# Block 0 of x loaded as plain rows and transposed on TensorE, in a gated attention and token-MLP kernel

## The chip, the cores and the metric

The kernel runs on one core of a Trainium2 chip. The metric is the device time in microseconds (us) of one execution; of several runs the median counts. The core has five engines with instruction streams of their own: TensorE (PE in the profile, PEld for its weight loads), VectorE (DVE), ScalarE (ACT), GpSimd (POOL) and SyncE (SP). SP and ACT also issue DMA transfers.

## The reference, cut to what matters

```python
x = A_x                                        # (1, 2048, 512) bf16
g = sigmoid((x * gate_w).sum(-1, keepdims=True))
qkv = x @ wqkv                                 # 512 -> 3*512, 32 heads of 16
# each position attends to 8 positions: itself and 2, 4, .. 14 before it
a = softmax(q . k[pos - 2w], masked where pos - 2w < 0) . v[pos - 2w] @ wo
h = layernorm(x, axis=-1)                      # over the 512 channels
u = gelu(einsum("bsd,sf->bdf", h, w1) + b1)    # token mixing, F = 1792
y = einsum("bdf,fs->bds", u, w2) + b2
out = g * a + (1 - g) * transpose(y)
```

The matmuls are the projections of q, k and v, the two of the token MLP, the output projection, and small ones that sum products over a head.

## The kernel before, in words

The sequence of 2048 positions is cut into 16 tiles of 128 (t, or st) and into 4 blocks of 512 (sb). Block 0 is tiles 0 to 3. x is held in SBUF twice. `X` has positions on the partitions and is used for the layernorm and the MLP. `XT` has channels on the partitions: four channel groups dt of 128, each 2048 positions long; it is the moving operand of the q, k and v projections.

**How the order is made.** Nothing is executed where it is written. `A` (`_Sched.add`, L88) and `sch.dma` (L114) record operations with an engine, a planned duration, and the names that they read and write. `_pass` (L146) is a list scheduler: it gives each engine a fixed order from planned durations. A DMA's end is planned from its bytes (L210 to L213), or set by hand in `lands` (L214). `chain(...)` (L924) forces an order on the operations named. `plan_waits` (L235) turns dependencies into semaphore waits. At run time each engine follows its list; an operation whose operands are late holds up all that stands behind it on that engine. [...]

**The start.** GpSimd writes a tile of ones (L421) and makes the identity matrix from it (L422). VectorE clears a tile, `warm0` (L525), and sums the identity to the indicator `RP` (L429). TensorE runs nine matmuls of that zero tile, `warm1` (L527 to L535), 128x512 each. Their result is used by nothing.

Meanwhile ACT's queue loads the first channel group of q's weights (`ld_w(0, 0, 1, "act")`, 128 KB), and SP's queue issues in this order (L477 to L491): two transposing loads that fill `XT` for positions 0 to 383 and 384 to 511 (`ld_xt0`, L472); channel group 1 of q's weights (128 KB); groups 2 and 3 (256 KB); all of k's weights (512 KB); a transposing load of block 1 (`ld_xt`, L465); X tiles 0 to 3 and 4 to 7 (`ld_x`, 512 KB each); the transposing loads of blocks 2 and 3; X tiles 8 to 11 and 12 to 15; v's weights. From there on a load waits until the fifth load before it in a list has landed (`throttle`, L438).

**Projections of block 0** (L613 to L619). q has four outputs (dl 0 to 3) in PSUM banks 0 to 3, k has four in banks 4 to 7. TensorE runs for the four q banks: channel group 0 for positions 0 to 383 (four 128x384 matmuls), group 0 for 384 to 511 (four 128x128), group 1 (four 128x512), groups 2 and 3 (eight 128x512). Then come the four k banks (sixteen 128x512). Here "the k projections" means those sixteen. After them TensorE goes on with blocks 1 to 3, v, and so on (L623 to L637). ScalarE copies each finished bank to SBUF (L606, L609).

**After the projections.** VectorE multiplies q by shifted k (`qkm`, L668), and TensorE sums the products over heads (`qkr`, L676), in bursts of 32 matmuls put between its other work. Layernorm statistics are `ln1` (L553, one per tile) and `ln2`; ScalarE normalises (`ln3`, L577). The MLP's matmuls are L794 and L844. The softmax follows on VectorE and ScalarE, then the weighted sum of v (L779 to L784), then the output projection on TensorE (`wo`, L860) and the combination on VectorE (`cmb`, L881). VectorE's order is written out in one chain (L940 to L946): `warm0`, `rp`, statistics of tiles 0 to 3, `qkm_0_0_0`, `qkm_0_1_0`, statistics of tiles 4 to 7, and so on.

Of the kernel before, what the change touches and what calls it, by code (L numbers as in the profile page):

```python
# [27 lines left out]
OUTQ = "sp"  # L28
XS = 384
HT0 = 12  # L30


class _Op:
# [256 lines left out]
def _views(nc, es):  # L290
    off = {}
    cur = [0]

    def region(name, nbytes):
        nbytes = (nbytes + 63) // 64 * 64
        off[name] = cur[0]
        cur[0] += nbytes

    region("X", NST * D * 2)
    region("XT", 4 * S * 2)  # L300
    region("WQKV", 4 * 3 * D * 2)
    region("W1W", 4 * NST * 256 * 2)
    region("PBUF", 2 * 4 * S * 2)
    region("WO", 4 * D * 2)
    region("Q5", 4 * S * 2)
    region("K5", 4 * KROW * 2)
    region("V5", 4 * KROW * 2)
    region("ATX", 8 * NW * HC * 2)
    region("ATT", NW * SC * 2)
    region("OUTS", 4 * D * 2)  # L310
    region("BR", 128)
    region("BT", 128)
    region("IDENT", 128 * 2)
    region("ONES", 128 * 2)
    region("RP", 32 * 2)
    region("SMALL", 2048)
    total = cur[0]
    arena = es.enter_context(nc.sbuf_tensor("arena", [128, total], U8))

    def view(name, dtype, dims, extra=0):  # L320
        base = arena[:].bitcast(dtype)
        pstride = base.ap[0][0]
        esz = mybir.dt.size(dtype)
        assert off[name] % esz == 0
        return bass.AP(base.tensor, off[name] // esz + extra, [[pstride, 128]] + [list(d) for d in dims])

    def pview(name, dtype, p0, np_, dims, extra=0):
        base = arena[:].bitcast(dtype)
        pstride = base.ap[0][0]
        esz = mybir.dt.size(dtype)  # L330
        return bass.AP(base.tensor, p0 * pstride + off[name] // esz + extra, [[pstride, np_]] + [list(d) for d in dims])

    return view, pview, off, total


def bass_gated_mix__sliding_local_dilated__mixer_token_mlp__prompt_kernel(nc, A_x, A_wqkv, A_wo, B_x, B_w1, B_b1, B_w2, B_b2, gate_w, out, dbg=None):
    with contextlib.ExitStack() as es:
# [32 lines left out]
        ATT = view("ATT", BF16, [(NW * HC, 2), (HC, NW), (1, HC)])  # L370
        T1 = view("X", BF16, [(D, NST), (1, D)])
        IDENT = view("IDENT", BF16, [(1, 128)])
        ONES = view("ONES", BF16, [(1, 128)])
        RP = view("RP", BF16, [(1, 32)])
        M4 = view("PBUF", FP32, [(4 * HC, 2), (HC, 4), (1, HC)], extra=0)
        M2 = view("PBUF", FP32, [(2 * HC, 2), (HC, 2), (1, HC)], extra=8 * HC)
# [38 lines left out]
        def psub(ap_, p0, np_, offs, dims):  # L415
# [2 lines left out]

        A = sch.add

        c_ones = A("pool", lambda e: e.memset(ONES, 1.0), 0.3, writes=["ones"], name="ones")  # L421
        c_ident = A("pool", lambda e: e.affine_select(out=IDENT, in_=ONES, pattern=[[1, 128]], compare_op=ALU.is_equal,  # L422
                                                     fill=0.0, base=0, channel_multiplier=-1),
                    0.4, reads=["ones"], writes=["ident"], name="ident")
        A("pool", lambda e: e.memset(sub(K5, 0, [(KROW, 4), (1, PAD)]), 0.0), 0.2, writes=["k5pad"], name="k5pad")
        A("pool", lambda e: e.memset(sub(V5, 0, [(KROW, 4), (1, PAD)]), 0.0), 0.2, writes=["v5pad"], name="v5pad")
        def f_rp(e):
# [5 lines left out]
        def mk_dma(dst, src):  # L433
            return lambda e: e.dma_start(dst, src)  # L434
# [17 lines left out]
        def ld_w(tn, d0, n, q="sp"):  # L452
            ds = sch.dsem("wqkv%d_%d" % (tn, d0))
            op = sch.dma(q, mk_dma(WQKV[:, d0:d0 + n, tn * D:(tn + 1) * D], wqkv_v[:, d0:d0 + n, tn * D:(tn + 1) * D]),
                         n * 128 * D * 2, ds, writes=["wqkv%d_%d" % (tn, dt) for dt in range(d0, d0 + n)],
                         deps=throttle() if q == "sp" and n == 4 else [], after=prev_dma() if q == "sp" else [],
                         issue=0.65 if n == 4 else 0.45, name="d_wp%d_%d" % (tn, d0))
            if q == "sp":
                init_dmas.append(op)
            return op  # L460
# [8 lines left out]
        def ld_xt0(s0, s1):  # L469
            ds = sch.dsem("xt0_%d" % s0)  # L470
            dst = XT[:, :, s0:s1]
            op = sch.dma("sp", lambda e: e.dma_start_transpose(dst, x2d[s0:s1, :]), (s1 - s0) * D * 2, ds, issue=1.25,  # L472
                         writes=["xt_%d" % t for t in range(s0 // 128, s1 // 128)], after=prev_dma(), name="d_xt0_%d" % s0)
            init_dmas.append(op)
            return op

        first_loads = [ld_w(0, 0, 1, "act"), ld_xt0(0, XS), ld_xt0(XS, 512), ld_w(0, 1, 1), ld_w(0, 2, 2), ld_w(1, 0, 4)]  # L477
        for op_ in first_loads[4:]:
            op_.deps -= set(init_dmas)
        ld_xt(1)  # L480
        init_dmas[-1].deps -= set(init_dmas)
        for op_, t_ in zip(first_loads + [init_dmas[-1]], (2.3, 3.95, 4.5, 4.8, 5.6, 7.2, 9.2)):
            op_.lands = t_
        del init_dmas[2]
        ld_x(0, 4)
        ld_x(4, 4)
        ld_xt(2)
        ld_xt(3)
# [32 lines left out]
        A("act", lambda e: e.activation(out=B1C, in_=BT[:, 0, 0:NFT], func=AF.Copy), 0.2, reads=["btc"], writes=["b1c"], name="b1c")  # L521
        A("act", lambda e: e.activation(out=B2C, in_=BT[:, 1, 0:NST], func=AF.Copy), 0.2, reads=["btc"], writes=["b2c"], name="b2c")

        WARM = view("OUTS", BF16, [(1, D)], extra=0)
        A("dve", lambda e: e.memset(WARM, 0.0), 0.2, writes=["outs0"], name="warm0")  # L525

        def f_warm(n):  # L527
            def fn(e):
                ins = None
                for _ in range(n):  # L530
                    ins = e.matmul(ps[:, 7, :], lhsT=WARM[:, 0:128], rhs=WARM, start=True, stop=True)
                return ins
            return fn

        last_tx = A("pe", f_warm(9), 4.0, reads=["outs0"], writes=["lg7_0", "lg7_1"], name="warm1", prio=-100)  # L535

        ALLXT = ["xt_%d" % t for t in range(NST)]

        JK = view("OUTS", BF16, [(1, D)], extra=0)
        def cols(v_, lo, n, step=1):  # L540
# [9 lines left out]
        for hf in range(2):  # L550
            t0 = 8 * hf
            for t in range(t0, t0 + 8):
                A("dve", (lambda t_: (lambda e: e.bn_stats(out=ST6[:, t_, :], in_=X[:, t_, :])))(t), 0.59,  # L553
                  reads=["x%d" % t], writes=["st6_%d" % t], name="ln1_%d" % t, prio=0)
            sr = ["st6_%d" % t for t in range(t0, t0 + 8)]
            h8 = (lambda v_: cols(v_, t0, 8))
            A("dve", (lambda t0_: (lambda e: e.tensor_tensor(out=mv(t0_, 0, 2), in0=st6(t0_, 1, 8, 2), in1=st6(t0_, 4, 8, 2), op=ALU.add)))(t0),
# [53 lines left out]
        tnames = ["q", "k", "v"]  # L611
        first = [(tn, dl) for tn in range(2) for dl in range(4)]
        fbn = [["acc%d" % b] for b in range(4)] + [["lg%d_0" % b, "lg%d_1" % b] for b in range(4, 8)]  # L613
        for (b0, d0, d1, s0, s1) in ((0, 0, 1, 0, XS), (0, 0, 1, XS, 512), (0, 1, 2, 0, 512), (0, 2, 4, 0, 512), (4, 0, 4, 0, 512)):
            for b in range(b0, b0 + 4):
                tn, dl = first[b]
                last_main[0] = A("pe", f_proj(tn, dl, 0, b, d0, d1, s0, s1), 0.216 * (d1 - d0) * (s1 - s0) / 512,
                                 reads=ALLXT[s0 // 128:s1 // 128] + ["wqkv%d_%d" % (tn, dt) for dt in range(d0, d1)],
                                 writes=fbn[b], after=[last_main[0]], name="pf_%s%d_%d_%d" % (tnames[tn], dl, d0, s0))  # L619
        for b, (tn, dl) in enumerate(first):  # L620
            A("act", f_evq(tn, dl, 0, b), 0.52, reads=fbn[b] + (["k5pad"] if tn == 1 else []),
              writes=["%s5_%d_0" % (tnames[tn], dl)], name="ev_%s%d_0" % (tnames[tn], dl), prio=0)
# [188 lines left out]
        for ft in range(NFT):  # L811
            j = ft // 2
            emit_ph2(ft, (2, 3) if ft < 3 else (0, 1, 2, 3))
            bank = p2bank[ft]
            A("act", (lambda ft_, bank_: (lambda e: e.activation(out=UT[:, ft_, :], in_=ps[:, bank_, :], func=AF.Gelu_apprx_tanh,  # L815
                                                                bias=col(B1C, ft_))))(ft, bank), 0.72,
              reads=["acc%d" % bank, "b1c"], writes=["ut%d" % ft] + ALLXT,
              name="gel_%d" % ft, prio=0)
            if ft % 2 == 1 and j + 4 <= 6:
                ld_w1(j + 4)  # L820
# [103 lines left out]
        def chain(names):  # L924
            for a_, b_ in zip(names, names[1:]):
                byname[b_].order.add(byname[a_])

        def ln1(*ts):
            return ["ln1_%d" % t for t in ts]

        def ln2(hf):
            return ["ln2%s%d" % (c_, hf) for c_ in "abcd"]
# [4 lines left out]
        def lnr(hf):  # L937
            return ["ln_rstd%d" % hf, "ln_nmr%d" % hf]

        chain(["warm0", "rp"] + ln1(0, 1, 2, 3) + ["qkm_0_0_0", "qkm_0_1_0"] + ln1(4, 5, 6, 7) + ln2(0)  # L940
              + ["qkm_0_2_0"] + lnr(0) + ["qkm_0_3_0", "qkm_0_0_2"] + ln1(8, 9) + ["qkm_0_1_2"] + ln1(10, 11, 12) + ["qkm_0_2_2"] + ln1(13, 14)
              + ["qkm_0_3_2", "qkm_1_0_0"] + ln1(15) + ln2(1) + ["t_b", "qkm_1_1_0"] + lnr(1)
              + ["qkm_1_2_0", "msk_0", "sm_ma0", "sm_mb0", "qkm_1_3_0"] + gz(12, 13, 14, 15, 0, 1) + [
# [6 lines left out]
        def atn(u):  # L950
# [1 line left out]

        chain(["avm_2", "g_omg", "g_c2", "g_g", "ava_0"])
        chain(["ph3b_14"] + ["wo_%d" % i for i in range(4)] + ["ph3a_15", "ph3b_15", "wo_4"])
        chain(["ln3_%d" % t for t in range(8, 16)] + ["gel_0", "gel_1"] + ["lev_1_%d" % w for w in range(4)] + ["sm_pre", "sm_exp0", "sm_exp1", "gel_2", "gel_3", "gel_4"] + atn(0) + ["gel_5"] + atn(2) + ["gel_6"] + atn(1) + ["gel_7"] + atn(3)
              + ["gel_8", "g_tanh", "gel_9"] + atn(4) + ["gel_10"] + atn(6) + ["gel_11", "gel_12"] + atn(5) + ["gel_13"] + atn(7) + ["t1_0"])

        if dbg is not None and "keep" in dbg:
            keepf = dbg["keep"]
# [92 lines left out]
```

## Time and profile before

| | us |
|---|---|
| median of 3 runs | 170.05 |
| the runs | 169.89, 170.05, 170.68 |
| the profiled execution | 169.85 |
| its span, first to last instruction | 168.0 |

| engine | busy us | share of the span |
|---|---|---|
| PE | 163.9 | 98% |
| DVE | 150.8 | 90% |
| ACT | 75.5 | 45% |
| POOL | 1.0 | 1% |

A time in the profile counts from the first instruction. A `q` behind an engine's name (SPq, ACTq) means its instruction queue, where DMAs are issued. A matmul's listed duration runs past the start of the next one, since matmuls are pipelined; the distance from start to start is what one costs in a row of them. `x12` after a group is its number of instructions, and `[0.25 <-DMA ...]` is idle time before it and what ended that.

### The profile page before, as it was taken

What the parts mean: (1) busy time and instruction counts of PE and PEld (TensorE: products, weight loads), DVE (VectorE), ACT (ScalarE), POOL (GpSimd) and SP (SyncE); (2) the same over time, 40 slices, a digit from 0 to 9 for tenths busy, and PEclk for the clock granted to TensorE, in tenths of its full rate; (3) what the DMA queues carried; (4) which work ended last, traced back from release to release, by engine and by line L of the source; (5) the groups of instructions that cost most, each with busy time, mean ns of one, the idle gap of its engine ahead of it and who ended that gap; (6) DMA issues with size and microseconds to landing.
All of it is one profiled execution on the core that took longest, in us unless ns stands there. A gap on an engine that the chain in (4) does not pass through costs nothing.

```text
span 168.0 us, 2160 instructions
## 1 busy us (share of the span) xinstructions
PE 163.9 (98%) x861; PEld 77.4 (46%) x861; DVE 150.8 (90%) x154; ACT 75.5 (45%) x115; POOL 1.0 (1%) x9
## 2 busy tenths in 40 slices
PE   7999999999999999999999999999999999999993
PEld 2455555544454444444444444444444444444462
DVE  1009999999999998799999999999999999999995
ACT  3177788898979938791231221131221312310000
POOL 2000000000000000000000000000000000000000
PEclk9999999999999999999999999999999999999999
DMA  6899999956303999555889906472573470000554
GB/s 143 255 295 248 290 326 292 297 171 192 125 0 101 358 295 288 143 162 137 191 219 329 327 19 149 104 210 65 162 218 99 119 222 0 0 0 0 184 180 140
DMA packets 47593, 29.64 MB, mean 176 GB/s; under 512 B 9824, under 2 KB 46432, under 8 KB 47584
## 3 DMA queue, kind: packets, MB, share of 16 engines
q1 hardware_dynamic: 45760, 25.11, 54.2%
q10 hardware_dynamic: 1824, 4.39, 9.9%
q8 instruction: 7, 0.11, 0.3%
q14 instruction: 2, 0.02, 0.0%
HBM read 21.11 MB, written 2.10 MB: 138 GB/s over the span
## 4 chain that ended last, share of the span: by engine, by line
PE 92%; DVE 2%; SPq 2%; DMA 2%; issue 0%
PE ps L794 29%; PE ps L844 29%; PE ps L598 24%; PE ps L860 6%; PE ps L676 4%; DVE arena L881 2%; DMA arena<-in_A_wqkv_dram 2%; SPq L472 2%; SPq L434 0%
## 5 line engine op out<-in xcount | busy, mean ns | idle before, releaser
L794 PE MATMUL ps<-arena 128*128 128x512 bf16 x224 | 48.9, 379 | 0.0
L844 PE MATMUL ps<-arena 128*128 128x512 bf16 x224 | 48.7, 379 | 0.0
L598 PE MATMUL ps<-arena 128*128 128x512 bf16 (+2 forms) x196 | 42.2, 375 | 0.2 <-DMA arena<-in_A_wqkv_dram 0.2
L668 DVE TENSOR_TENSOR arena<-arena 128x4096 bf16<-128x4096 bf16 (+1 forms) x12 | 35.6, 2990 | 0.0
L779 DVE TENSOR_TENSOR arena<-arena 128x8192 bf16<-128x8192 bf16 x8 | 35.0, 4418 | 0.0
L794 PEld LDWEIGHTS ps<-arena 128*128 128x128 bf16 x224 | 21.8, 98 | 26.8 <-issue 0.8
L844 PEld LDWEIGHTS ps<-arena 128*128 128x128 bf16 x224 | 21.9, 98 | 26.4
L598 PEld LDWEIGHTS ps<-arena 128*128 128x128 bf16 x196 | 21.7, 113 | 20.8 <-DMA arena<-in_A_wqkv_dram 0.9
L911 ACT ACTIVATE arena<-ps,arena 128x512 bf16<-128x512 f32 x16 | 12.5, 778 | 39.4 <-PE ps L844 39.4
L782 DVE TENSOR_TENSOR arena<-arena 128x4096 bf16<-128x4096 bf16 (+1 forms) x16 | 27.0, 1751 | 0.0
L609 ACT ACTIVATE arena<-ps 128x512 bf16<-128x512 f32 x32 | 18.9, 596 | 5.4 <-PE ps L598 5.2
L815 ACT ACTIVATE arena<-ps,arena 128x512 bf16<-128x512 f32 x14 | 9.6, 688 | 24.7 <-PE ps L794 22.2
L553 DVE BATCH_NORM_STATS2 arena<-arena 128x6 f32<-128x512 bf16 x16 | 10.0, 680 | 11.2 <-DMA arena<-in_A_x_dram 11.2
L860 PE MATMUL ps<-arena 128*128 128x512 bf16 (+1 forms) x80 | 14.2, 336 | 0.0
L606 ACT ACTIVATE arena<-ps 128x512 bf16<-128x512 f32 x16 | 9.0, 597 | 7.2 <-PE ps L598 7.2
L577 ACT ACTIVATE arena<-arena 128x512 bf16<-128x512 bf16 x16 | 12.0, 804 | 0.0
L881 DVE SCALAR_TENSOR_TENSOR arena<-ps,arena 128x512 bf16<-128x512 f32 (+1 forms) x20 | 11.5, 637 | 0.4 <-PE ps L860 0.2
L860 PEld LDWEIGHTS ps<-arena 128*128 128x128 bf16 x80 | 7.8, 98 | 6.2
L652 DVE SCALAR_TENSOR_TENSOR arena<-arena 128x512 bf16<-128x512 bf16 x16 | 9.9, 687 | 0.0
L726 DVE TENSOR_TENSOR arena<-arena 128x512 bf16<-128x512 bf16 (+4 forms) x11 | 7.3, 667 | 1.2 <-ACT arena L745 0.8
L676 PE MATMUL ps<-arena 128*32 128x512 bf16 x128 | 7.6, 380 | 0.0
L784 DVE TENSOR_TENSOR arena<-arena 128x1024 bf16<-128x1024 bf16 x8 | 5.5, 688 | 0.1
(40 smaller groups left out, 38.2 us busy)
## 6 DMA issues: line engine op xcount, KB each, us to landing
arena<-in_B_w_dram SPq DMA_DIRECT2D x7, 1024.0 KB, 8.7
arena<-in_B_w_dram SPq DMA_DIRECT2D x8, 896.0 KB, 5.1
arena<-arena ACTq DMA_DIRECT2D x32, 128.0 KB, 2.8
arena<-in_A_x_dram SPq DMA_DIRECT2D x5, 512.0 KB, 5.1
out_dram<-arena SPq DMA_DIRECT2D x15, 128.0 KB, 1.7
arena<-in_A_x_dram SPq DMA_DIRECT2D x1, 1536.0 KB, 8.4
arena<-in_A_wqkv_dram SPq DMA_DIRECT2D x2, 512.0 KB, 5.5
arena<-in_A_wo_dram SPq DMA_DIRECT2D x1, 512.0 KB, 8.5
```

The source lines that it names most:

```text
L577: A("act", (lambda t_: (lambda e: e.activation(out=X[:, t_, :], in_=X[:, t_, :], func=AF.Identity, scale=col(RSTD, t_), bias=col(NMR, t_)) ...
L598: ins = e.matmul(ps[:, bank, s0:s1], lhsT=lhsT, rhs=XT[:, dt, sb * 512 + s0:sb * 512 + s1], start=(dt == 0 and s0 == 0), stop=(dt == 3))
L609: return lambda e: e.activation(out=dst, in_=ps[:, bank, :], func=AF.Copy)
L668: return lambda e: e.tensor_tensor(out=PBL[buf][:, :, 512 * c0:512 * (c0 + nc_)], in0=in0, in1=in1, op=ALU.mult)
L676: ins = e.matmul(ps[32 * c:32 * c + 32, 4 + wl, :], lhsT=RP, rhs=PBL[buf][:, wl, c * 512:(c + 1) * 512], start=(dl == 0), stop=(dl == 3), ...
L779: A("dve", (lambda o_, i0, i1: (lambda e: e.tensor_tensor(out=o_, in0=i0, in1=i1, op=ALU.mult)))(pv, in0, in1), 4.4, reads=v_res + ["atx_% ...
L782: A("dve", (lambda pv_, n__: (lambda e: e.tensor_tensor(out=pv_[:, 0:n__], in0=pv_[:, 0:n__], in1=pv_[:, n__:2 * n__], op=ALU.add)))(pv, n ...
L794: ins = e.matmul(ps[:, bank, :], lhsT=W1W[:, slot, st, 128 * e_:128 * e_ + 128], rhs=X[:, st, :], start=(st == 0), stop=(st == NST - 1))
L844: ins = e.matmul(ps[:, bank, :], lhsT=W2S[slot][:, ft, 128 * e_:128 * e_ + 128], rhs=UT[:, ft, :], start=(ft == 0), stop=(ft == NFT - 1))
L860: ins = e.matmul(ps[:, bank, 0:c1 - c0], lhsT=OT[:, t, 128 * i:128 * i + 128], rhs=WO[:, t, c0:c1], start=(t == 0), stop=(t == 3))
L881: A("dve", (lambda i_, b_, c0_, c1_: (lambda e: e.scalar_tensor_tensor(out=T1[:, i_, c0_:c1_], in0=ps[:, b_, 0:c1_ - c0_], scalar=col(G, i ...
L911: A("act", (lambda i_, bank_: (lambda e: e.activation(out=T1[:, i_, :], in_=ps[:, bank_, :], func=AF.Identity, scale=col(OMG, i_), bias=co ...
```

## The change

It has these parts.

- The two transposing loads of block 0 go, and so does the load of X tiles 0 to 3 that came later. `ld_xr` loads tiles 0 and 1 in halves of 64 partitions, one half on SP's queue and one on ACT's, and tiles 2 and 3 whole on SP's. Groups 0 and 1 of q's weights come after tiles 0 and 1, group 0 on SP and group 1 on ACT.
- `f_tx`: TensorE multiplies the X tile (as weights) by the identity, one 128x128 matmul for each channel group, 16 in all, into banks 4 to 7. `f_xtc`: VectorE copies channel groups 0 and 1 of a tile from PSUM to `XT`, ScalarE groups 2 and 3.
- Groups 0 and 1 of the q projections of block 0 are cut into four position tiles: 32 matmuls of 128x128 in place of four each of 128x384, 128x128 and 128x512. Groups 2 and 3 and the k projections stay.
- The idle matmuls at the start read a constant 1.0 that the preamble has written, broadcast; they are six in place of nine, with one of 256 columns after the transposes of tile 1. VectorE's clearing of a tile and GpSimd's tile of ones go.
- VectorE's chain: the four copies, then the statistics of tiles 0 to 7, then `qkm_0_0_0`.
- ScalarE's chain: `gel_1` (a gelu of the MLP) comes after the four `lev_1` copies, not before them. The planner's landing times for the first loads are new, and those loads wait for no other load.

```diff
-        first_loads = [ld_w(0, 0, 1, "act"), ld_xt0(0, XS), ld_xt0(XS, 512), ld_w(0, 1, 1), ld_w(0, 2, 2), ld_w(1, 0, 4)]
...
+        def ld_xr(t, p0, p1, q):
+            ds = sch.dsem("x%d_%d" % (t, p0))
+            src = x2d[128 * t + p0:128 * t + p1, :]
+            return sch.dma(q, mk_dma(X[p0:p1, t, :], src), (p1 - p0) * D * 2, ds, issue=0.45, writes=["x%d" % t if p0 == 0 else "x%d_b" % t],
+                           name="d_x%d_%d" % (t, p0))
+        first_loads = [ld_xr(0, 0, 64, "sp"), ld_xr(0, 64, 128, "act"), ld_xr(1, 0, 64, "sp"), ld_xr(1, 64, 128, "act"),
+                       ld_w(0, 0, 1), ld_w(0, 1, 1, "act"), ld_xr(2, 0, 128, "sp"), ld_xr(3, 0, 128, "sp"), ld_w(0, 2, 2), ld_w(1, 0, 4)]
         ld_xt(1)
...
-        ld_x(0, 4)
         ld_x(4, 4)
...
-        last_tx = A("pe", f_warm(9), 4.0, reads=["outs0"], writes=["lg7_0", "lg7_1"], name="warm1", prio=-100)
+        CONE = nc.const_aps.tensor(1.0, [128, D], BF16)
+        def f_warm(n, w_=D):
...
+                    ins = e.matmul(ps[:, 0, 0:w_], lhsT=CONE[:, 0:128], rhs=CONE[:, 0:w_], start=True, stop=True)
+        def f_tx(t, h):
...
+                for dt in (2 * h, 2 * h + 1):
+                    ins = e.matmul(ps[:, 4 + 2 * (t % 2) + h, 128 * dt:128 * dt + 128], lhsT=X[:, t, 128 * dt:128 * dt + 128], rhs=IDENT,
+                                   start=(dt == 2 * h), stop=(dt == 2 * h + 1))
+        last_tx = A("pe", f_warm(NWARM), 0.427 * NWARM, writes=["acc0"], name="warm1", prio=-100)
+        em_tx(0)
+        em_tx(1)
+        A("pe", f_warm(1, 256), 0.2, writes=["acc0"], name="warm2")
+        em_tx(2)
+        em_tx(3)
...
-        for (b0, d0, d1, s0, s1) in ((0, 0, 1, 0, XS), (0, 0, 1, XS, 512), (0, 1, 2, 0, 512), (0, 2, 4, 0, 512), (4, 0, 4, 0, 512)):
+        for t in range(4):
+            em_pf(0, 0, 2, 128 * t, 128 * t + 128)
+        em_pf(0, 2, 4, 0, 512)
+        em_pf(4, 0, 4, 0, 512)
...
-        chain(["warm0", "rp"] + ln1(0, 1, 2, 3) + ["qkm_0_0_0", "qkm_0_1_0"] + ln1(4, 5, 6, 7) + ln2(0)
+        chain(["rp"] + ["xtc_%d_0" % t for t in range(4)] + ln1(*range(8)) + ["qkm_0_0_0", "qkm_0_1_0"] + ln2(0)
...
+        chain(["warm1"] + ["tx_%d_%d" % (t, h) for t in range(2) for h in range(2)] + ["warm2"]
+              + ["pf_q%d_0_0" % b for b in range(4)] + ["tx_%d_%d" % (t, h) for t in (2, 3) for h in range(2)] + ["pf_q0_0_128"])
```

## The prediction

> **What bounds the kernel now.** I read the page first: its busy times and the shares of the chain that ended last.
>
> ```profile
> PE 163.9 (98%) x861; PEld 77.4 (46%) x861; DVE 150.8 (90%) x154; ACT 75.5 (45%) x115; POOL 1.0 (1%) x9
> ...
> PE 92%; DVE 2%; SPq 2%; DMA 2%; issue 0%
> ```
>
> Then the chain in order of time (start, duration, what), and who TensorE waited for:
>
> ```profile
> 0.81 1.36 SPq L472
> ...
> 2.22 1.25 SPq L472
> ...
> 4.14 2.97 DMA arena<-in_A_wqkv_dram
> ...
> 7.15 26.95 PE ps L598 x124
> ...
> 161.97 3.98 DVE arena L881 x9
> ```
>
> ```profile
> PE ps L531 <- DVE arena L525: 1.3, 1, 1.3
> PE ps L598 <- DMA arena<-in_A_wqkv_dram: 0.2, 1, 0.2
> ```
>
> After 7.15 TensorE never waits: 124 matmuls take 26.95, 0.217 each, and so it goes to 161.9. So one number decides: when TensorE starts the k projections of block 0. All behind them is the same work in both kernels. Now that is 7.15 + 8 x 0.216 = 8.88; the timeline has 8.91:
>
> ```profile
> 1.25 3.91 PE L531 MATMUL ps<-arena 128*128 128x512 bf16 x9 [1.25 <-DVE arena L525]
> ...
> 5.00 1.91 PE L598 MATMUL ps<-arena 128*128 128x384 bf16 x12
> ```
>
> ```profile
> 8.91 3.62 PE L598 MATMUL ps<-arena 128*128 128x512 bf16 x16
> ```
>
> VectorE shows one long idle time, before the first statistics, and waits 0.2 at the very end for TensorE:
>
> ```profile
> 12.90 2.47 DVE L553 BATCH_NORM_STATS2 arena<-arena 128x6 f32<-128x512 bf16 x4 [11.21 <-DMA arena<-in_A_x_dram]
> 15.29 4.48 DVE L668 TENSOR_TENSOR arena<-arena 128x4096 bf16<-128x4096 bf16 x2
> 19.68 2.46 DVE L553 BATCH_NORM_STATS2 arena<-arena 128x6 f32<-128x512 bf16 x4
> ```
>
> So VectorE is close behind TensorE, but TensorE ends last.
>
> **The prices.** The nine idle matmuls start 0.424 apart (1.25 to 4.64, the start of the ninth), the sixteen k matmuls 0.216 apart ((3.62 - 0.38) / 15): TensorE's clock is slow at first. The ninth lasts 0.52, the others 0.63, so the change falls near 4.9. The page's row of granted clock shows 9 throughout and does not tell this. Four 128-column matmuls with their weight loads run from 5.65 to 5.87: 0.055 each, fast. Slow, I take a quarter of 0.424: 0.106.
>
> **TensorE's start, step by step.** The idle matmuls need no tile cleared by VectorE. VectorE's own first instruction, behind the same barrier, is at 0.92; I let TensorE start at 0.9 in place of 1.25 (0.8 to 1.25 are the ends). Six take 6 x 0.424: 3.44. Eight transposes of tiles 0 and 1: 8 x 0.106, 4.29. The 256-column idle matmul: 0.21, 4.50. Eight projections of tile 0: four slow to about 4.9, four fast, 5.14. Eight transposes of tiles 2 and 3: 0.44, 5.58. 24 projections of tiles 1 to 3: 1.32, 6.90. Groups 2 and 3, unchanged: 8 x 0.216, 8.63. The k projections start at **8.63** instead of 8.91: 0.28 earlier. The transposes, the idle matmul and the 32 small projections stand against twelve matmuls that went from 5.00 to 6.9; what is won is the wait for transposing loads, what is paid is their work on TensorE.
>
> **Do the loads come in time?** The DMA view of the first 9 us (slices of 0.225) has the first bytes at 1.8, and plain loads from 4.7 to 8.2 move 274 GB/s:
>
> ```profile
> GB/s 0 0 0 0 0 0 0 0 123 159 312 296 276 290 290 291 264 198 242 137 38 74 205 282 132 150 341 346 273 150 291 373 400 360 396 339 291 237 289 291
> ```
>
> ```profile
> 4.70:8.20 3.50, 3.25 (x19) 1.69 (x18) 0.00 (x0) 0.39 (x1) 0.00 (x0) 1.00 0.91 274
> ```
>
> A load of 128 KB on ACT's queue, issued at 0.82, lands 2.1 later: first bytes at 1.8, 0.5 of moving at 274 GB/s, so 0.6 for filling up and landing. Then with n blocks of 128 KB ahead and including a load, it lands at 1.8 + 0.48 n + 0.6: tile 0 at 2.9, tile 1 at 3.4, q groups 0 and 1 (n = 4) at 4.3, tile 2 at 4.8, tile 3 at 5.3, q groups 2 and 3 (n = 8) at 6.2, k (n = 12) at 8.2. TensorE wants them at 3.44, 3.9, 4.50, 5.14, 5.36, 6.90 and 8.63. All fit, tile 3 by 0.06. SP issues plain loads in 0.43 to 0.58 each, so tile 3 is issued at about 0.8 + 4 x 0.5 = 2.8 and k at 3.8 (now 4.61), ahead of their bytes. Were tile 3 as long from issue to landing as q groups 2 and 3 are now (3.0), it would land at 5.8, and k would start at 5.8 + 0.22 + 1.32 + 1.73 = 9.07, 0.16 later than now.
>
> **The copies.** VectorE copies 128x256 from PSUM; its nearest rows, the halves of L881, have 0.48. ScalarE's 128x512 copies have 0.60. Taken at 0.5, tile 3's copy on VectorE is done by 5.47 + 0.2 + 2 x 0.5 = 6.7 even right behind tile 2's; its projections come at 6.46 to 6.90. The ends are 0.3 and 0.75 each; the longer would cost 0.5 if both fell behind one another. I take 0, since tile 2's copy can start earlier. ScalarE is idle from 2.5 to 7.8 (a wait of 5.3), and its two more DMA issues (0.39 each) only move its table load of 1.28 to about 2.1 to 3.4, before its first copy.
>
> **VectorE's statistics.** Tiles 0 to 3 (2.47) and four copies (2.0) fall in idle time: nothing. Tiles 4 to 7 (2.46) move ahead of `qkm_0_0_0`. Their load takes the ring place of the load of tiles 0 to 3, which landed at 12.9; everything ahead ends some 0.6 earlier: 12.3. With 2.46 that gives 14.8; today `qkm` starts at 15.29. From 19.68 on VectorE is 0.5 + 2.46 = 3.0 ahead. This is worth nothing by itself, as TensorE bounds; it is spent in longer waits for ScalarE and TensorE. It is what lets VectorE follow, since its margin is 0.2 now. GpSimd's missing tile of ones (0.2) brings the identity earlier than the 1.37 at which it is done now; it is wanted at 3.44. SP's later transposing loads move up by about 0.8, at nothing: TensorE wants block 1 at 8.63 + 16 x 0.216 = 12.1. The moved gelu waits for a bank that TensorE wants only some 10 us later: nothing.
>
> **Sum.** The profiled execution took 169.85 with its span of 168.0: 1.85 lies outside and stays. 169.85 - 0.28 = 169.57. The median of the runs shown stands 0.20 above that execution, so I say **169.8** for the median.
>
> [...] The row here is 0.055 for a 128-column matmul with its weight load, and these transposes are ordinary matmuls by an identity; I go by the row. [...]
>
> **Rivals.**
> - *Faster: loads quick, clock early.* The row above reaches 400 GB/s; at 380 the tiles land at 2.4 + 0.345 n, tile 3 at 4.5 and k at 6.5. Were the clock fast from 3.44 on too, TensorE's steps sum to 0.44 + 0.11 + 0.44 + 0.44 + 1.32 + 1.73 = 4.48, and k starts at 7.92: 1.0 earlier, 169.05 for the median. Against it: the plain loads averaged 274, and the clock has been slow for 3.7 us.
> - *Slower: the clock opens late.* Short matmuls with waits between them may not open it as nine long ones did. If all 40 small matmuls behind 4.50 ran slow: 4.50 + 40 x 0.106 + 1.73 = 10.47, 1.56 later, 171.6. Were groups 2 and 3 slow too, 1.7 more: the far end. It decides from an opening at about 7.3 on, where k starts at 9.76. For it: six idle matmuls in place of nine; against it: TensorE has work without a planned gap from 0.9 on.
> - *Waits that the planner did not see.* TensorE's order is fixed. Its first `qkr` burst starts at 34.04, and the product it needs ends at 30.87 + 2.27 = 33.14: 0.9 of margin. Planned with VectorE 3.0 earlier, it waits if tiles 4 to 7 land late: at 14.2 as now, 1.9 late, less the margin, 1.0 is lost: 170.8. A late tile 3 belongs here too.
>
> **How the numbers follow.** Half a per cent, 0.85, is about what a measurement of this kernel can tell from no change. The forecast, with 169.3 to 170.5 of its own for the copies, the loads and the clock's moment: 0.54. The faster rival: 0.19. The late clock: 0.17. The waits: 0.10, of which 0.04 over 170.9. So faster 0.19, same 0.54 + 0.06 = 0.60, slower 0.17 + 0.04 = 0.21. The range from 168.9 to 171.3 leaves out the far half of the late clock and the end of the faster rival.
>
> **What would show it.** In the profile after: idle matmuls from 0.9, 0.42 apart; transposes from 3.4; the eight matmuls of groups 2 and 3 without a wait for weights; k projections from 8.6; no wait of TensorE behind them; VectorE's `qkm` at 14.8 and longer waits at L720 and L726. It is wrong if TensorE waits for tile 3 or k's weights, if small matmuls stay 0.106 apart beyond 5, or if a burst of L676 waits.

## The result, and the profile after

Measured side by side, 17 runs each, the changed kernel has a median of 172.26 us (170.58 to 174.21) and the kernel before 170.39 (169.89 to 171.11). The ratio is 1.0087, with a 95% interval of 1.0061 to 1.0113: slower, by something under one per cent. The ratio leaves out the four runs of the changed kernel above 173.3, which are counted as slow (the median of the other thirteen is 171.69); that is why it is less than the quotient of the two medians, 1.011.

The profiled execution of the changed kernel took 171.23, 1.38 more than that of the kernel before; its span grew from 168.0 to 169.5. First its page, busy times and the shares of the chain that ended last:

```profile
PE 164.9 (97%) x895; PEld 78.9 (47%) x895; DVE 152.3 (90%) x157; ACT 76.5 (45%) x119; POOL 0.7 (0%) x8
...
PE 90%; DMA 4%; DVE 2%; SPq 2%; issue 0%
```

TensorE still bounds, but two per cent of the span have gone from PE to DMA. The chain in order of time (start, duration, what) says which DMA:

```profile
0.80 0.57 SPq L432
...
1.42 0.58 SPq L432
...
2.04 0.58 SPq L432
...
4.09 6.23 DMA arena<-in_A_wqkv_dram
...
10.36 22.64 PE ps L633 x104
...
163.47 3.98 DVE arena L923 x9
```

L432 is a plain load's issue, L633 a projection. The transfer of 6.23 is k's weights: issued at 4.09, landed at 10.32. So the k projections start at **10.36**, where the kernel before has 8.91 and the forecast had 8.63. That is 1.45 later, of 1.5 in the span. TensorE's timeline of the changed kernel shows what came before:

```profile
0.84 2.72 PE L537 MATMUL ps<-const-bfloat16-1.0 128*128 128x512 bf16 x6 [0.84 <-PEq L1082]
3.38 0.60 PE L545 MATMUL ps<-arena 128*128 128x128 bf16 x4
4.25 0.58 PE L545 MATMUL ps<-arena 128*128 128x128 bf16 x4 [0.26 <-DMA arena<-in_A_x_dram]
4.62 0.42 PE L537 MATMUL ps<-const-bfloat16-1.0 128*128 128x256 bf16 x1
5.18 0.69 PE L633 MATMUL ps<-arena 128*128 128x128 bf16 x8
5.70 0.39 PE L545 MATMUL ps<-arena 128*128 128x128 bf16 x4
6.83 0.38 PE L545 MATMUL ps<-arena 128*128 128x128 bf16 x4 [0.75 <-DMA arena<-in_A_x_dram]
7.05 13.21 PE L633 MATMUL ps<-arena 128*128 128x128 bf16 x77
```

L545 are the transposes. Those of tile 0 came on time, those of tile 1 waited 0.26, and tile 3 came so late (landed 6.70) that TensorE stood for 0.75. Without any wait for k it would have reached k at 6.83 + 0.22 + 24 x 0.056 + 8 x 0.216 = 10.12; k's own landing put 0.24 on top. So tile 3 by itself costs 1.2, and k's weights by themselves the whole 1.45: both loads are late by about as much.

VectorE's view, to set against that of before:

```profile
7.14 0.42 DVE L554 CAST arena<-ps 128x256 bf16<-128x256 f32 x1 [0.71 <-PE ps L545]
7.49 2.46 DVE L588 BATCH_NORM_STATS2 arena<-arena 128x6 f32<-128x512 bf16 x4
14.80 2.47 DVE L588 BATCH_NORM_STATS2 arena<-arena 128x6 f32<-128x512 bf16 x4 [4.85 <-DMA arena<-in_A_x_dram]
17.19 4.48 DVE L710 TENSOR_TENSOR arena<-arena 128x4096 bf16<-128x4096 bf16 x2
```

The copies (0.42) and the statistics of tiles 0 to 3 do lie in what was idle time. But tiles 4 to 7 landed at 14.78, so `qkm` starts at 17.19, 1.9 later than the 15.29 of before. SP's queue shows why: their load stands behind the transposing load of block 1 (L463), whose issue lasted until 10.08.

```profile
4.60 5.48 SPq L463 DMA_TRANSPOSE arena<-in_A_x_dram  x1
10.13 0.58 SPq L432 DMA_DIRECT2D arena<-in_A_x_dram  x1
```

In the kernel before the same issue was over at 8.46:

```profile
5.12 3.34 SPq L465 DMA_TRANSPOSE arena<-in_A_x_dram  x1
```

Since the eight statistics lie behind it by then, VectorE comes to its next small operations at 21.59 against 22.18 before: 0.6 ahead, where 3.0 was forecast.

### The profile page after: what moved, and what is told of

The parts are those of the page before. It is cut to its first block, busy times and chain, and to the rows that moved or that the text cites. A ratio compares the mean times of both kernels' runs of the same rounds, so it can differ in the third digit from the quotient of the medians.

```text
span 169.5 us, 2242 instructions
## 1 busy us (share of the span) xinstructions
PE 164.9 (97%) x895; PEld 78.9 (47%) x895; DVE 152.3 (90%) x157; ACT 76.5 (45%) x119; POOL 0.7 (0%) x8
## 3 DMA queue, kind: packets, MB, share of 16 engines
q10 hardware_dynamic: 1984, 4.52, 10.4%
## 4 chain that ended last, share of the span: by engine, by line
PE 90%; DMA 4%; DVE 2%; SPq 2%; issue 0%
PE ps L836 29%; PE ps L886 29%; PE ps L633 23%; PE ps L902 6%; PE ps L718 4%; DMA arena<-in_A_wqkv_dram 4%; DVE arena L923 2%; SPq L432 2%
## 5 line engine op out<-in xcount | busy, mean ns | idle before, releaser
L633 PE MATMUL ps<-arena 128*128 128x512 bf16 (+1 forms) x216 | 42.7, 356 | 0.2
L633 PEld LDWEIGHTS ps<-arena 128*128 128x128 bf16 x216 | 22.4, 114 | 20.2 <-ACT arena L612 0.8
L902 PE MATMUL ps<-arena 128*128 128x512 bf16 (+1 forms) x80 | 14.2, 336 | 0.0
L612 ACT ACTIVATE arena<-arena 128x512 bf16<-128x512 bf16 x16 | 12.2, 805 | 0.0
```

Source lines behind the costliest of these rows:

```text
L612: A("act", (lambda t_: (lambda e: e.activation(out=X[:, t_, :], in_=X[:, t_, :], func=AF.Identity, scale=col(RSTD, t_), bias=col(NMR, t_)) ...
L633: ins = e.matmul(ps[:, bank, s0:s1], lhsT=lhsT, rhs=XT[:, dt, sb * 512 + s0:sb * 512 + s1], start=(dt == 0 and s0 == 0), stop=(dt == 3))
L902: ins = e.matmul(ps[:, bank, 0:c1 - c0], lhsT=OT[:, t, 128 * i:128 * i + 128], rhs=WO[:, t, c0:c1], start=(t == 0), stop=(t == 3))
```

## The experiments

One view is enough to compare them: when the k projections start. In the profiled executions in which nothing else waits, span less this start is a constant: 168.0 - 8.91 = 159.1 before, 169.5 - 10.36 = 159.1 after, 168.4 - 9.23 = 159.2 in e5, 168.7 - 9.74 = 159.0 in e3, 169.1 - 9.96 = 159.1 in e7, 169.7 - 10.56 = 159.1 in e1, 169.9 - 10.80 = 159.1 in e12, 169.1 - 9.98 = 159.1 in e10, 171.4 - 12.2 = 159.2 in e6, 172.0 - 12.9 = 159.1 in e9, 171.0 - 11.9 = 159.1 in e8; in e2 it is 171.3 - 11.41 = 159.9, with a later wait of 0.76 in it. (Where a row of the timeline begins with the eight matmuls of groups 2 and 3, k starts 8 x 0.216 behind it; in e5 k follows from the first `qkr` burst, which comes 33.00 - 10.36 = 22.64 after it, as in the changed kernel. In e2, e6, e8 and e9 k is counted off from the starts of single matmuls in the trace.)

| kernel | tile 3 landed | k landed | k start | median | ratio to before, 95% |
|---|---|---|---|---|---|
| before | - | 8.71 | 8.91 | 170.39 | 1 |
| after | 6.70 | 10.32 | 10.36 | 172.26 | 1.0061 to 1.0113 |
| e1 block 1 plain | 6.21 | 10.52 | 10.56 | 171.44 | 1.0041 to 1.0111 |
| e2 block 1 after k | 7.16 | 9.93 | 11.41 | 172.91 | 1.0132 to 1.0188 |
| e3 whole, one queue | 5.52 | 9.22 | 9.74 | 170.61 | 1.0011 to 1.0035 |
| e5 whole, two queues | 5.75 | 9.18 | 9.23 | 170.63 | 0.9994 to 1.0035 |
| e6 halves, one queue | 7.37 | 10.80 | 12.2 | 172.44 | 1.0115 to 1.0170 |
| e7 fewer loads | 5.62 | 9.51 | 9.96 | 170.64 | 1.0009 to 1.0059 |
| e9 changed, VectorE's old order | 7.81 | 10.63 | 12.9 | 172.84 | 1.0075 to 1.0168 |
| e10 e5, VectorE's old order | 5.82 | 9.54 | 9.98 | 170.68 | 1.0002 to 1.0035 |
| e12 halves by channel | 5.85 | 10.39 | 10.80 | 171.24 | 1.0033 to 1.0074 |

(Times other than the medians are from one profiled execution each. TensorE's clock was slow from 7.1 to 10.5 in e6's and from 8.4 to 11.8 in e9's.)

Three theories stood at first. A: the transposing load of block 1, issued behind k's weights, holds the loads ahead of it up. B: the loads of tiles 0 and 1 as they are now made cost it, either since they are cut in two (B1) or since they go by two queues (B2). The third: VectorE's new order costs it.

### e1, e2: the load behind

e1 loads block 1 by a plain load:

```diff
-            op = sch.dma("sp", lambda e: e.dma_start_transpose(dst, x2d[sb * 512:(sb + 1) * 512, :]), 512 * D * 2, ds,
+            op = sch.dma("sp", (lambda e: e.dma_start(dst, x2d[512:1024, :].rearrange("(a p) d -> p a d", p=128))) if sb == 1 else
+                         (lambda e: e.dma_start_transpose(dst, x2d[sb * 512:(sb + 1) * 512, :])), 512 * D * 2, ds,
```

> The changed kernel, with the transposing load of block 1 replaced by a plain load of the same 512 KB into the same place (block 1 of XT then holds x in the wrong layout, so the projections of block 1 are of other numbers). Theory A (the transposing load behind the plain loads on SP's queue holds them up, while its descriptors are made and when its first packets stand behind k's weights): X tile 3 lands near 5.5 instead of 6.70, k's weights near 8.3 instead of 10.32, the k projections start near 8.9 and the time is about that of the kernel before, 170.4 of the median. Theory B (the plain loads themselves are slow, because tiles are cut in halves and issued on two queues at once; the transposing load plays no part): tile 3 stays near 6.7, k's weights near 9.5 to 10.3, and the time stays at 171.5 to 172.3.

Measured: 171.44 against 170.36, ratio 1.0076 (1.0041 to 1.0111). e2 lets that load wait until k's weights have landed:

```diff
+        first_loads[10].deps.add(first_loads[9])
```

> The changed kernel, with the transposing load of block 1 issued only when k's weights have landed. Theory A: tile 3 near 5.5, k's weights near 8.3, the k projections near 8.9; block 1 then lands near 12.3, about when TensorE wants it (16 x 0.216 after the k projections start), so the time is 170.4 to 170.9. Theory B: tile 3 near 6.7, k's weights near 10, block 1 near 14, and TensorE waits for both: 172.5 to 173.5, slower than the changed kernel.

Measured: 172.91, ratio 1.0160 (1.0132 to 1.0188). In both, tile 3 (6.21, 7.16) and k's weights (10.52, 9.93) are still late, with no transposing load in flight beside tile 3. Theory A falls as the main cause. Tile 3 is 0.5 earlier in e1, and k's weights 0.4 earlier in e2, than in the changed kernel, so a small part is not excluded. In e2 the delayed queue also makes tiles 4 to 7 late (16.87), and TensorE's timeline has the wait that the prediction named as its third rival:

```profile
34.69 1.91 PE L719 MATMUL ps<-arena 128*32 128x512 bf16 x32 [0.76 <-DVE arena L711]
```

### e3, e5, e6: halves or queues

e3 loads tiles 0 and 1 whole and everything by SP's queue:

```diff
-        first_loads = [ld_xr(0, 0, 64, "sp"), ld_xr(0, 64, 128, "act"), ld_xr(1, 0, 64, "sp"), ld_xr(1, 64, 128, "act"),
-                       ld_w(0, 0, 1), ld_w(0, 1, 1, "act"), ld_xr(2, 0, 128, "sp"), ...
+        first_loads = [ld_xr(0, 0, 128, "sp"), ld_xr(1, 0, 128, "sp"),
+                       ld_w(0, 0, 1), ld_w(0, 1, 1), ld_xr(2, 0, 128, "sp"), ...
```

> The changed kernel, with the four X tiles of block 0 loaded whole and all first loads on SP's queue (nothing on ACT's). Theory A: tile 3 and k's weights are as late as in the changed kernel (about 6.7 and 10.3), 172. Theory B: issues take 0.43 each again, tile 3 lands by 5.6 and k's weights by 8.8, the k projections start near 9.0, 170.5.

Measured: 170.61, ratio 1.0023 (1.0011 to 1.0035); most of the loss is gone. e5 and e6 separate the two things that e3 undid. e5, whole tiles on two queues:

```diff
-        first_loads = [ld_xr(0, 0, 64, "sp"), ld_xr(0, 64, 128, "act"), ld_xr(1, 0, 64, "sp"), ld_xr(1, 64, 128, "act"),
+        first_loads = [ld_xr(0, 0, 128, "sp"), ld_xr(1, 0, 128, "act"),
```

> The changed kernel with tiles 0 and 1 loaded whole, tile 0 on SP's queue and tile 1 on ACT's; group 1 of q's weights stays on ACT's queue. The one-queue run had brought 170.6. Theory B1 (the cutting in halves, with more and smaller loads, is what costs): as fast as with one queue, 170.5 to 170.8, tile 3 by 5.6, k's weights by 9.3. Theory B2 (two queues at once put the DMA engines out of step, and each load then waits for the last engine): as slow as the changed kernel, 171.5 to 172.3, tile 3 at 6 or later, k's weights near 10.

Measured: 170.63 against 170.16, ratio 1.0014 (0.9994 to 1.0035). e6, halves on one queue:

```diff
-        first_loads = [ld_xr(0, 0, 64, "sp"), ld_xr(0, 64, 128, "act"), ld_xr(1, 0, 64, "sp"), ld_xr(1, 64, 128, "act"),
-                       ld_w(0, 0, 1), ld_w(0, 1, 1, "act"), ld_xr(2, 0, 128, "sp"), ...
+        first_loads = [ld_xr(0, 0, 64, "sp"), ld_xr(0, 64, 128, "sp"), ld_xr(1, 0, 64, "sp"), ld_xr(1, 64, 128, "sp"),
+                       ld_w(0, 0, 1), ld_w(0, 1, 1), ld_xr(2, 0, 128, "sp"), ...
```

> The changed kernel with tiles 0 and 1 in halves, but all first loads on SP's queue. Theory B1: slow, 171.5 to 172.3. Theory B2: near the run with whole tiles on one queue, later only by two more issues of 0.43 each, so at most 0.9: 170.6 to 171.5, with k's weights near 9.5 and the engines of a load landing within 0.3 of each other.

Measured: 172.44, ratio 1.0142 (1.0115 to 1.0170). So it is the cutting in halves (e5 against the changed kernel, e3 against e6), and with whole tiles the second queue costs nothing that shows: B1. The views of SP's own queue show one part of how. First the changed kernel (start, duration of the group, what):

```profile
0.80 1.20 SPq L432 DMA_DIRECT2D arena<-in_A_x_dram  x2
2.04 0.58 SPq L432 DMA_DIRECT2D arena<-in_A_wqkv_dram  x1
2.67 0.90 SPq L432 DMA_DIRECT2D arena<-in_A_x_dram  x2
```

The same view of e6:

```profile
0.79 2.47 SPq L432 DMA_DIRECT2D arena<-in_A_x_dram  x4
3.31 1.06 SPq L432 DMA_DIRECT2D arena<-in_A_wqkv_dram  x2
4.41 0.91 SPq L432 DMA_DIRECT2D arena<-in_A_x_dram  x2
```

And of e3:

```profile
0.80 0.87 SPq L432 DMA_DIRECT2D arena<-in_A_x_dram  x2
1.72 0.90 SPq L432 DMA_DIRECT2D arena<-in_A_wqkv_dram  x2
2.66 0.91 SPq L432 DMA_DIRECT2D arena<-in_A_x_dram  x2
```

SP takes 0.58 or so for a half of 64 partitions (four in 2.47), and 0.39 to 0.43 for a whole tile of twice the bytes. ACT's queue took 1.47 for its two halves. So half the bytes take longer to issue than all of them, and in e6, where the four halves stand one behind another, tile 3 is issued at 4.89 instead of 3.14. From 1.5 to 3.0 the DMA engines are less busy than with whole tiles (0.41 in the changed kernel and 0.28 in e6, against 0.66 in e3 and 0.73 in e5). The windows from 1.5 to 3.0 and from 3.0 to 4.7 show it in their last two columns, the busy share of the DMA engines and GB/s. The changed kernel:

```profile
1.50:3.00 1.50, 1.50 (x5) 0.44 (x3) 0.00 (x1) 0.06 (x1) 0.00 (x0) 1.00 0.41 114
3.00:4.70 1.70, 1.44 (x11) 0.81 (x9) 0.47 (x2) 1.60 (x2) 0.00 (x0) 1.00 0.91 243
```

The same windows of e6:

```profile
1.50:3.00 1.50, 1.50 (x5) 0.44 (x3) 0.00 (x0) 0.58 (x1) 0.00 (x0) 1.00 0.28 63
3.00:4.70 1.70, 0.93 (x6) 0.24 (x4) 0.42 (x1) 0.38 (x1) 0.00 (x0) 1.00 0.37 109
```

And of e3:

```profile
1.50:3.00 1.50, 1.50 (x5) 0.44 (x3) 0.00 (x1) 0.58 (x1) 0.00 (x0) 1.00 0.66 185
3.00:4.70 1.70, 1.62 (x11) 1.00 (x9) 0.85 (x2) 0.64 (x2) 0.00 (x0) 1.00 0.85 249
```

And of e5:

```profile
1.50:3.00 1.50, 1.50 (x5) 0.46 (x3) 0.00 (x1) 1.27 (x1) 0.00 (x0) 1.00 0.73 181
3.00:4.70 1.70, 1.53 (x17) 0.86 (x16) 0.76 (x2) 0.67 (x3) 0.00 (x0) 1.00 0.91 298
```

By 4.7 the changed kernel has moved 114 x 1.5 + 243 x 1.7 = 584 KB, e3 has 701, e6 has 280 and e5 has 778.

That is not all. In the changed kernel and in e3 tile 3 is issued in the same slot (the second of the pair from 2.66 on), and it still lands 1.2 apart. The trace has sixteen moments for each load, one for each share of it, and the landing is the last of them: 6.70, 5.52 and 7.81 for tile 3 in the changed kernel, in e3 and in e9 (below, the same first loads as the changed kernel). That a share is the part of one of the 16 DMA engines that the page counts is the author's reading; the trace does not name the engine.

```
after  5.42 5.51 5.54 5.55 5.57 5.58 5.60 5.60 5.61 5.64 5.76 5.77 6.41 6.43 6.61 6.70
e3     5.09 5.13 5.14 5.18 5.19 5.20 5.21 5.23 5.29 5.30 5.32 5.35 5.36 5.36 5.38 5.52
e9     5.46 5.52 5.53 5.56 5.62 5.62 5.64 5.65 5.76 5.97 6.71 7.50 7.55 7.64 7.71 7.81
```

The eighth share is done at 5.60 against 5.23; that fits the slow start. From the eighth to the last there are 1.1 in the changed kernel, 0.6 in e1, 1.5 in e2 and 2.2 in e9, against 0.3 in e3, 0.8 in e5 and 1.0 in e10. But e6, which has the halves too, shows 0.4, and so does e12 (below). So some shares fall behind, by up to 2.2 where halves of 64 partitions go by two queues (e9); the cut alone does not bring it, and whole tiles do not exclude it. Why those shares fall behind was not settled. The prediction's formula, which counted bytes alone, had left this spread out.

### e12: halves of another form

Halves by channel, 128 partitions of 256 channels, on two queues as in the change:

```diff
-            src = x2d[128 * t + p0:128 * t + p1, :]
-            return sch.dma(q, mk_dma(X[p0:p1, t, :], src), ...
+            src = x2d[128 * t:128 * t + 128, 4 * p0:4 * p1]
+            return sch.dma(q, mk_dma(X[:, t, 4 * p0:4 * p1], src), ...
```

> The changed kernel with tiles 0 and 1 cut in halves by channel (128 partitions x 256 channels) instead of by partition (64 x 512); the queues and the number of loads are those of the changed kernel. If the form with 64 partitions is what makes an issue take 0.57 to 0.83: issues of 0.4 to 0.45, tile 3 issued at 2.7 to 2.8 and landing near 6, k's weights near 9.4, 170.8 to 171.2. If it is the number of loads and their halved size: as the changed kernel, 171.8 to 172.4.

Measured: 171.24 against 170.24, ratio 1.0053 (1.0033 to 1.0074). The issues are short again (0.87 for SP's two), and tile 3 lands at 5.85. The first of the windows, in e12, is no longer slow (GB/s last):

```profile
1.50:3.00 1.50, 1.50 (x5) 0.46 (x3) 0.00 (x1) 0.79 (x1) 0.00 (x0) 1.00 0.77 184
```

So the slow start (114 in the changed kernel, 184 here) belongs to the 64-partition form, not to the number of loads. But q's groups 2 and 3 are late: ten shares by 6.59, the other six from 7.94 to 8.94; TensorE waits 1.33 for them, and k lands at 10.39. That shares fall behind is not shown to come from the smaller loads: in e7 and e10, with whole tiles, the last share of the same load is 2.1 and 1.8 behind the eighth, here 2.6. Its ratio lies between those of e5 and of the changed kernel, but the interval overlaps both, so how the loss divides between the two parts is not measured well.

### e7: fewer, larger loads

Tiles 0 and 1 whole, q's groups 0 and 1 in one load, tiles 2 and 3 in one load, all on SP:

```diff
+        first_loads = [ld_xr(0, 0, 128, "sp"), ld_xr(1, 0, 128, "sp"),
+                       ld_w(0, 0, 2), ld_x23(), ld_w(0, 2, 2), ld_w(1, 0, 4)]
```

> One queue and fewer loads: tile 0, tile 1, groups 0 and 1 of q's weights in one load, tiles 2 and 3 in one load, groups 2 and 3, k. Both theories: not slower than the one-queue run, 170.3 to 170.6. If what is left is the time of the bytes (1.5 MB before k's weights are in, in every version), k's weights land near 9 whatever the cutting, and the time is that of the kernel before within 0.3.

Measured: 170.64, ratio 1.0034 (1.0009 to 1.0059). No gain over e3 and e5. Of q's groups 2 and 3, fifteen shares were done by 6.33 and the last at 8.09, so TensorE waited 0.59 and k started at 9.96.

### e4, e9, e10: VectorE's order

e4 is the kernel before with only the rest of the change: idle matmuls that read the constant, and VectorE's new order.

```diff
-        chain(["warm0", "rp"] + ln1(0, 1, 2, 3) + ["qkm_0_0_0", "qkm_0_1_0"] + ln1(4, 5, 6, 7) + ln2(0)
+        chain(["rp"] + ln1(*range(8)) + ["qkm_0_0_0", "qkm_0_1_0"] + ln2(0)
```

> The kernel before, with only the rest of the change: the nine idle matmuls read the constant, and VectorE's order has the statistics of tiles 0 to 7 ahead of the first product. Loads and projections are those of before. Both theories: the k projections start at 8.9 as before and the time is within 0.3 of the kernel before, 170.4. A third view (VectorE's order itself costs time: products start near 17.4 instead of 15.3 since tiles 4 to 7 land at 14.2, and a burst of TensorE waits for them): slower by 0.5 to 1.0.

Measured: 171.16, ratio 1.0060 (1.0033 to 1.0087). Here the statistics of eight tiles stand ahead of `qkm`, and tiles 4 to 7 land at 14.86. VectorE's timeline of e4:

```profile
13.21 4.84 DVE L552 BATCH_NORM_STATS2 arena<-arena 128x6 f32<-128x512 bf16 x8 [11.54 <-DMA arena<-in_A_x_dram]
17.97 4.48 DVE L667 TENSOR_TENSOR arena<-arena 128x4096 bf16<-128x4096 bf16 x2
```

TensorE's timeline of e4:

```profile
33.39 1.91 PE L675 MATMUL ps<-arena 128*32 128x512 bf16 x32 [0.66 <-DVE arena L667]
```

`qkm` starts 2.7 later than before, and TensorE's first burst waits 0.66 for it: VectorE's order costs by itself, without the early tiles 0 to 3. Another 0.3 of e4's loss comes ahead of that and is not VectorE's: k's weights, loaded as in the kernel before, landed at 9.18 in this execution, and k starts at 9.22. Is VectorE's order part of the loss of the whole change? e9 is the changed kernel with VectorE's old order, e10 is e5 with it:

```diff
-        chain(["rp"] + ["xtc_%d_0" % t for t in range(4)] + ln1(*range(8)) + ["qkm_0_0_0", "qkm_0_1_0"] + ln2(0)
+        chain(["rp"] + ["xtc_%d_0" % t for t in range(4)] + ln1(0, 1, 2, 3) + ["qkm_0_0_0", "qkm_0_1_0"] + ln1(4, 5, 6, 7) + ln2(0)
```

> The changed kernel with VectorE's order of before: statistics of tiles 4 to 7 behind the second product. The run with only the rest of the change was 0.6% slower than the kernel before, with a wait of TensorE for VectorE ahead of the first burst. If that order is a second cause of the changed kernel's loss (its slower executions, where tiles 4 to 7 land late): 171.3 to 171.8 and less spread, since TensorE's late start by 1.45 stays. If the late loads are the only cause: 172.0 to 172.5 as the changed kernel.

> Tiles loaded whole on two queues (170.63 against 170.16 in its call), and VectorE's order of before. With one queue or two, k's weights landed at 9.2 against 8.71 in the kernel before, so the k projections start 0.3 later. If VectorE's order costs nothing once the loads are quicker: 170.4 to 170.7, within 0.3% of the kernel before. If it costs in some executions: at the kernel before's time or up to 0.2 under it, with less spread.

Measured: e9 172.84, ratio 1.0121 (1.0075 to 1.0168), no better than the changed kernel; e10 170.68, ratio 1.0018 (1.0002 to 1.0035), like e5. With tiles 0 to 3 done early VectorE's order costs nothing that shows. The loss is in the loads.

### e8, e11: the loads of the kernel before

e8 gives the kernel before its q weights by ACT's queue:

```diff
-        first_loads = [ld_w(0, 0, 1, "act"), ld_xt0(0, XS), ld_xt0(XS, 512), ld_w(0, 1, 1), ld_w(0, 2, 2), ld_w(1, 0, 4)]
+        first_loads = [ld_w(0, 0, 1, "act"), ld_xt0(0, XS), ld_xt0(XS, 512), ld_w(0, 1, 1, "act"), ld_w(0, 2, 2, "act"), ld_w(1, 0, 4)]
```

> The kernel before, with all of q's weights on ACT's queue (groups 0, then 1, then 2 and 3), so that they need not wait behind the two transposing loads on SP's queue; k's weights stay on SP's. If the loads' order bounds the start: q's groups 2 and 3 land by 5.5 to 6.5 instead of 7.11, TensorE goes from 5.0 to the k projections without a wait, they start at 8.5, and the time is 0.2 to 0.45 under the kernel before. If the bytes bound it, or two queues put the engines out of step (theory B2): k's weights land at 8.7 or later, and the time is the same or up to 1 slower.

Measured: 170.50, ratio 1.0058 (1.0022 to 1.0095). Its runs fall in two groups, seven at 170.3 to 170.6 and four at 172.7 to 172.8, with one at 171.3. The profiled one was of the upper group; its two transposing loads landed at 6.42 and 7.43, where those of before landed at 4.83 and 5.35, and TensorE waited 1.28 for them. TensorE's timeline has a second loss:

```profile
6.56 3.99 PE L599 MATMUL ps<-arena 128*128 128x384 bf16 x13 [1.28 <-DMA arena<-in_A_x_dram]
```

Thirteen matmuls take 3.99 here, where the first twelve took 1.91 before, and those of 512 columns start 0.43 apart from 8.22 to 10.35: the clock was slow until about 10.4. So k starts at 11.9, 3.0 later than before. The late loads make 1.56 of this (6.56 against 5.00), and the other 1.4 go with the slow clock. One execution is shown, so whether the others of the upper group are like it, and what makes the loads late, is open. Nor did the weights gain much: q's groups 2 and 3 landed at 6.88, before at 7.11.

e11 splits the loads of the kernel before: q's groups 2 and 3 apart, k in two loads, TensorE's order to match.

```diff
-        ..., ld_w(0, 1, 1), ld_w(0, 2, 2), ld_w(1, 0, 4)]
+        ..., ld_w(0, 1, 1), ld_w(0, 2, 1), ld_w(0, 3, 1), ld_w(1, 0, 2), ld_w(1, 2, 2)]
```

> The kernel before, with groups 2 and 3 of q's weights loaded one by one, k's weights in two loads of 256 KB, and TensorE going by group (q group 2, q group 3, k groups 0 and 1, k groups 2 and 3). In the kernel before, TensorE waits 0.25 for q's groups 2 and 3. If a load's landing is what it waits for, the first of the two lands near 6.6, TensorE does not stop, and the time is 0.1 to 0.3 under the kernel before. If the bytes or the issues bound it (two more issues of 0.43 each): the same or up to 0.4 slower.

Measured: 170.37 against 170.24, ratio 1.0002 (0.9987 to 1.0017): nothing. No version here is faster than the kernel before. e5, the change without its halves, cannot be told from it; e3 and e10 stand 0.2 per cent above it.

## Why the prediction was wrong

The start of the k projections decides the time, as the prediction said; eleven executions have shown it above. The step that failed is "Do the loads come in time?", with its "All fit, tile 3 by 0.06". Tile 3 landed at 6.70 where 5.3 was put, k at 10.32 where 8.2 was put. Point by point:

- **"First bytes at 1.8, 0.5 of moving at 274 GB/s".** The rate was taken from a stretch in which loads of 128 to 512 KB over 128 partitions were already in flight, and used for the first loads, which the change cuts. From 1.5 to 3.0 it was 114. With whole tiles the count of bytes comes near: by 4.7 the formula has (4.7 - 1.8) x 274 = 795 KB, e5 moved 778, e3 701 and the changed kernel 584. For k it is short even then: 9.2 to 9.5 in the versions with whole tiles, where 8.2 was put. So about half of the 2.1 by which k came late does not come from the halves, and what it comes from is open.
- **"SP issues plain loads in 0.43 to 0.58 each".** This is in range: 0.58 for the halves. But ACT's second half took 0.83 or so (1.47 for two), and a half costs as much issue as a whole tile or more, which the prediction did not count against it. k was issued at 4.09, not 3.8.
- **0.6 for filling up and landing.** It came from one load of 128 KB with nothing ahead of it. Tile 3's sixteen shares came over 1.3. That this could be is in the prediction: tile 3 as long from issue to landing as the weights gave 5.8 and a k start of 9.07. It was 3.56 from issue to landing, and it is 3.6 in e5 too, but 2.4 in e3: that time is no constant. The case was priced 0.16 later than before, and shared with the waits of a burst a chance of 0.10, of which 0.04 lay over 170.9. A margin of 0.06 on a landing was no margin.
- **TensorE's prices.** Right. The idle matmuls start at 0.84 (0.9 was put), the transposes and small projections cost 0.107 each while the clock was slow and 0.056 after. The clock opened at 5.38 instead of 4.9 (the small projections start 0.106 apart at 5.24 and 0.056 apart from 5.42 on), which cost nothing, since TensorE waited for tile 3 after that.
- **The copies** at 0.5: 0.42 on VectorE, no wait for them in the profiled execution. Right. ScalarE's table load came at 2.94 instead of about 2.1, since ACT's three issues took 1.47 and 0.60; TensorE waited for nothing behind it.
- **VectorE's statistics.** "Everything ahead ends some 0.6 earlier: 12.3" counted on the loads ahead coming earlier and failed with them: the load of tiles 4 to 7 was issued at 10.13, after 8.51 and 9.14 for the two X loads of before, and landed at 14.78, `qkm` at 17.19 instead of 14.8. TensorE did not wait for it, as its own start was 1.45 later. The planner did move the first burst forward: 112 instead of 124 matmuls lie between the start of q's groups 2 and 3 and that burst. So VectorE's margin shrank, and e2 and e4 show the wait that can come of it.
- **The rivals.** "The clock opens late" was not it in the changed kernel's profiled execution; in e2's it opened only at 8.61, nine small matmuls were slow that would have been fast, 0.45. That the kind of work decides when the clock opens was the author's guess; no run varies it alone. "Loads quick" was wrong in its sign.

What is left open: the last 0.1 to 0.3 per cent of the versions with whole tiles. Their k lands at 9.2 to 9.5, against 8.71 before, with the same 1.5 MB up to k's end. One execution hardly tells these apart: e4, with the loads of the kernel before, has 9.18. In the kernel before the sixteen shares of q's groups 2 and 3 came within 0.54; in e3 they took 1.46, in e7 2.44, in e10 2.42. What held them closer together in the kernel before is not shown. k's own shares are no measure of it. Where a transposing load stands right behind k's, the last nine of them come within 0.11 in every kernel here, and the last one 0.3 or less after SP has issued that load (8.46 and 8.71 before, 9.04 and 9.22 in e3, 10.08 and 10.32 in the changed kernel); in e2, where it was issued later, they lie 2.1 apart. Whether the one holds up the other is open.

## What to carry to other kernels

Price a load on the path by its issue and its last share, not by its bytes at the mean rate: here the mean rate put tile 3 at 5.3, and it landed at 6.70, with 1.3 from its first share to its last. Read from a trace the issue time of the very form that is planned and that spread, and give a landing at least the spread as margin. The halves of 64 partitions, cut to have the first tiles sooner, came with tile 3 at 6.70 and k's weights at 10.32, where whole tiles on the same queues (e5) had 5.75 and 9.18. When one start decides the whole span, compare that start between kernels first; it tells more than one run's time does.

## What the runs showed of the hardware that was not expected

- A load of 64 partitions x 1 KB took 0.57 to 0.83 to issue (the changed kernel), one of 128 partitions x 1 KB 0.38 to 0.46, one of 128 x 512 bytes 0.39 to 0.46 (e12). The first load of 128 partitions behind such halves took 0.58 to 0.60 as well, and one behind two transposing loads 0.57 (the kernel before, at 3.52).
- In e9 and e6 the granted clock closed again soon after it had opened. In e9 TensorE waited 1.66 for tile 3; the windows (TensorE's busy time second, PEclk third from the end) show 1.39 of work in the first 3.41 with the fast clock, then half clock for as long, under full work:

```profile
4.97:8.38 3.41, 1.39 (x21) 1.16 (x21) 0.70 (x3) 0.72 (x3) 0.00 (x0) 1.00 0.77 160
8.38:11.80 3.42, 3.42 (x28) 2.60 (x26) 2.67 (x5) 0.56 (x2) 0.00 (x0) 0.50 1.20 258
11.80:15.00 3.20, 3.20 (x16) 1.69 (x15) 0.00 (x0) 2.77 (x6) 0.00 (x0) 1.00 1.00 225
```

  In e6 it was the same from 7.09 to 10.50 (PEclk 0.50), after a window with 1.51 of work. In the changed kernel the window from 5.38 on held 2.66 of work, and the clock stayed (PEclk 1.00). So in the two slowest profiled executions, 173.11 and 173.73, long waits for loads at the start and a slow clock behind them came together; that the waits bring the slow clock is not shown. The moment at which the clock opened differs between the executions: 3.5 or earlier in e5 (its transposes start 0.05 to 0.07 apart from there on), about 4.9 in the kernel before, 5.38 in the changed kernel and 8.61 in e2 (four transposes still take 0.59 there at 7.30, against 0.38 in the changed kernel at 6.83); in e8 the clock was slow until about 10.4.
- One share of a load came 1.8 after the other fifteen (e7, q's groups 2 and 3: 6.33 and 8.09).
